# Copies and adding transfers in both halves of experts 2 to 6, expert 1's second weights made earlier, and 48 instead of 60 weight conversions ahead of the last layer

## The chip, the cores and the metric

The kernel runs on one core of a Trainium2 chip. The metric is device time in microseconds (us) of one execution. Everything else in this document comes from the hardware profiler's record of one execution: its engines are PE (TensorE: matmuls; PEld, its weight loads), DVE (VectorE), ACT (ScalarE), POOL (GpSimd) and SP (SyncE), which here issues nearly all DMA transfers. PEclk is the clock that TensorE was granted, as a share of its full speed.

## The reference, cut to what matters

```python
x = attention(q, k, v)                    # 4 x 576 tokens = 2304, 8 heads of 64: local and strided masks
logits = x @ w_gate; P = np.exp(logits - logits.max())
for _ in range(8):                        # Sinkhorn: rows, columns
    P /= P.sum(1, keepdims=True) + 1e-09
    P /= P.sum(0, keepdims=True) + 1e-09
    P *= N / E
for e in range(8):                        # experts: 512 -> 1024 -> 512
    out += P[:, e:e+1] * (np.maximum(x @ w1[e], 0) @ w2[e])
xn = out / sqrt(mean(out**2) + 1e-6) * rms_g
g = xn @ w_gate2; val = xn @ w_val        # 512 -> 1536
result = (g * sigmoid(g) * val) @ w_out   # 1536 -> 512
```

All of it is float32. The four SwiGLU weights arrive as float64 and are turned into float32 on the chip.

## The kernel before

**Products.** A float32 product is made of three matmuls on values split into a high and a low part (ACT copies the high part, DVE subtracts to get the low one). Experts 1 to 7 and the last layer use a scheme of seven products for a 2 x 2 block matrix (k = 0 to 6) in place of eight.

**Stages.** Attention ends at 253 us and overlaps expert 0, which is computed plainly in chunks of 256 tokens and a last one of 512 (matmuls L725 to L727) until 337 us. The gate and the Sinkhorn rows and columns (L702 to L720, with small matmuls L711) lie around the start of expert 1. Experts 1 to 7 follow, from 325.5 to 1673 us in 42 groups, then the SwiGLU layer in three passes, 18 groups.

**A group** is (expert g, half hh of the hidden features, third qd of the tokens). An expert has six groups: hh = 0 with qd = 0, 1, 2, then hh = 1 with qd = 2, 1, 0. In this text they are its first to sixth group. A group has two rounds of seven slots; a slot is one first-layer product (six matmuls, L1152, into one of two banks called ub) whose result DVE or ACT takes out of the bank (DVE: L1184, L1258, ACT: L1295, L1303), splits (ACT L1177, DVE L1180), and leaves for the second layer. Behind each slot stands one second-layer unit of nine matmuls (L1752, into banks called db), which belongs to the slot 12 slots earlier (LAG = 12). So the second layer of a group lies mostly in the time of the group that follows it, and that of an expert's sixth group in the first group of the next expert. The next product of a bank waits until the bank has been read.

**Second-layer results.** When the unit of product k is complete, `evict_1` takes it to the accumulator acc: by an ACT copy (L1773) for hh = 0 and k in (0, 2, 3, 4), else by a DVE add (L1784; k = 5 is a double one of 128x1536). When both halves of an expert are in acc, `close_region` weighs the region with the gate (ACT, L1803, three of them) and `gather` adds it to a buffer in HBM (L1809, a transfer with accumulation that POOL issues); the next expert's copy then waits for the transfer. Expert 7 gets that buffer back by an adding transfer into acc.

**Weights.** `second_weights` loads a half's second-layer weights into a tile raw_2 (L1038), forms differences (DVE L1041) and splits them (ACT L1054, DVE L1057) product by product, in the group before. raw_2 has the tag "r", the place that last_w (expert 0's last weights) holds before it.

**Float64 weights.** `conversion` turns them into float32 in 72 pieces. A piece is a 256 KB load (L824 or L827), seven DVE instructions in four steps (L832, L833; L839, L843; L849, L850; L856) and a store to HBM (L860). There is one buffer, cv: the load of the next piece is issued when L850 of this one has read it. The queue conv hands out steps with a fixed number of ticks between them (CONV_WAIT; a tick is a slot's worth of work); CONV_EP pieces are handed out from expert 2 on, the others from the second group of the first pass on. `prepare_2` for a SwiGLU pass calls conv.drain, which at that place writes down every piece that is still missing up to the one it needs, step behind step.

**The last layer** starts with the normed tokens: `norm_turn` and `norm_blocks` (L1395 to L1453) make them out of acc and write them to HBM (SP, L1429 and L1453), and SP loads them back as blocks xt and xx (L1084), one per product. An instruction list per engine is fixed when the kernel is built: every engine works through its own in order.

Of the kernel before, what the change touches and what calls it, by code (L numbers as in the profile page):

```python
# [17 lines left out]
P = 128  # L18
# [95 lines left out]
def kernel(  # L114
# [45 lines left out]
    EARLY = 2  # L160
    EARLY_AT = (5, 6)
    SUMS = 24
    CONV_WAIT = (7, 12)
    CONV_EP = 60
    LAG = 12
    TURN_AT = (29, 30, 31, 32, 33, 34), (32, 33, 34, 35, 36, 37)
    BLOCK_LAG = (2.5, 1.6, 0.85)
# [855 lines left out]
    def w2_piece(k, r, s):  # L1023
        return w2t.rearrange("p f s n -> p f (s n)")[:, k, 512 * r + 256 * s : 512 * r + 256 * (s + 1)]

    def second_weights(g, hh):

        both = const.tile([P, 2048], F32, name="raw_2", tag="r")
        raw = [both[:, 1024 * r : 1024 * (r + 1)] for r in range(2)]
        b11, b12, b21, b22 = ([t[:, 256 * i : 256 * (i + 1)] for t in raw] for i in range(4))  # L1030
        new = [fa[:, 4608 + 256 * r : 4864 + 256 * r] for r in range(2)]
        t1, t3, t2, t4 = new, b12, b11, b21

        def load(r):
            f = 2 * hh + r
            for h in range(2):
                rows = w2[g][(f + h * (NF // 2)) * P : (f + h * (NF // 2) + 1) * P, :]
                nc.sync.dma_start(out=raw[r][:, 512 * h : 512 * (h + 1)], in_=rows)  # L1038

        def sub(out, a, b):  # L1040
            nc.vector.tensor_tensor(out=out, in0=a, in1=b, op=ALU.subtract)  # L1041

        def early(r):
            sub(t1[r], b12[r], b11[r])
            sub(t3[r], b22[r], b12[r])
            return 600

        def late(r):
            sub(t2[r], b22[r], t1[r])
            sub(t4[r], b21[r], t2[r])  # L1050
            return 600

        def high(k, r):
            nc.scalar.activation(w2_piece(k, r, 0), (b21, b11, t4, t2, t1, t3, b22)[k][r], AF.Copy)  # L1054

        def low(k, r):
            nc.vector.tensor_tensor(  # L1057
                out=w2_piece(k, r, 1), in0=(b21, b11, t4, t2, t1, t3, b22)[k][r],
                in1=w2_piece(k, r, 0).bitcast(F32), op=ALU.subtract,
            )  # L1060
            return 256

        def begin():
            prep2.add([(WRITE, lambda: load(0)), (0, lambda: load(1))])

        def product(k):
            steps = []
            if k == 0:
                steps += [(READ, lambda: early(0)), (STEP, lambda: early(1))]
            steps += [(1, lambda: [high(k, r) for r in range(2)].clear()), (1, lambda: sum(low(k, r) for r in range(2)))]  # L1070
            if k == 1:
                steps += [(1, lambda: late(0)), (1, lambda: late(1))]
            prep2.add(steps, ("w2", g, hh, k))

        return begin, product
# [386 lines left out]
    with tc.manual_schedule():  # L1462
# [182 lines left out]

        def down_tile(u, t):
            u.down(u, t)
            if not u.left and t == u.n // P - 1 and u.f == NF - 1:
                begin_2[0], product_2[0] = second_weights(1, 0)
                begin_2[0]()  # L1650
                for k in range(7):
                    product_2[0](k)

        for idx in range(-LOOK, n1 - LOOK):
            nxt = idx + LOOK
# [7 lines left out]
            if u.f == 0:  # L1663
                if "x" not in u.cell:
                    fetch(u)
                if u.left:
                    bg.add(gate(u.t0, u.n, u.cell["x"]), 20)
                    if u.at:
                        area = fa[:, :1280], fa[:, 1280:3328].bitcast(F32R)
                        steps = sums(0, us[0].cell["x"], *area) if u.at == 1 else []  # L1670
                        steps += sums(u.at, u.cell["x"], *area)
                        bg.add(steps, 30 if u.at == 1 else SUMS, tag="sums")
                else:
                    bg.drain()
                    begin_sbuf()
                    area = acc[:, 2].rearrange("p a n -> p (a n)")[:, :1280], hx.rearrange("p a n -> p (a n)")[:, :2048]
                    wgc2 = hx.rearrange("p a n -> p (a n)")[:, 2048:2560].rearrange("p (c n) -> p c n", c=KC)
                    gate_split(wgc2)
                    steps = []
                    for i in range(2):  # L1680
                        x = [t[:, :, i * TA : (i + 1) * TA] for t in u.cell["x"]]
                        steps += sums(u.at + i, x, *area)
                    bg.add(steps, 40, tag="sums")
                    load_1(1, 0)
                    for k in (0, 1, 4, 3, 5, 2):
                        load_block(xmap[k], False, 0, k)
            u.up(u)
# [73 lines left out]
        def evict_1(n, k):  # L1761
# [6 lines left out]
                ps = ps[:, :, None, :].to_broadcast([P, 3, 2, 256])  # L1768
            else:
                a = a[:, :, 256 * col : 256 * (col + 1)]  # L1770
            if hh == 0 and k in (0, 2, 3, 4):
                bg.drain(("expert", qd, half, col if half else None))
                nc.scalar.copy(a, ps)  # L1773
            elif (g, hh) == (E - 1, 1):
# [12 lines left out]
            if n % NQD == NQD - 1:  # L1787
                if n < NGP - 1:
                    product_2[at](k)
                elif k >= 3:  # L1790
                    prepare_2(E, (0, 2, 1, 3)[k - 3])
            if hh == (g < E - 1) and k in (1, 5, 6):
                close_region(g, qd, *((1, 0) if k == 1 else (0, None) if k == 5 else (1, 1)))
            if (g, hh) == (E - 1, 1) and k >= 5:
                scales[k - 5].add(norm_scale(qd, 3 * (k - 5)), ("scale", qd))
# [171 lines left out]
        def fetch_left(k):  # L1967
            for x in list(left):
                if x[3] == k or made(x[2], x[3]):
                    norm.drain(("plain" if x[3] < 3 else "blocks", x[2]))  # L1970
                    load_block(*x)
                    left.remove(x)

        xmap, free = nmap, nfree
        free, gone_x = free[:1], free[1]
        last_r = const.tile([P, 2048], F32R, name="last_r", tag="r")
# [163 lines left out]
```

## Time and profile before

| | us |
|---|---|
| median of 3 runs | 2172.15 (2170.27 to 2173.97) |
| profiled execution | 2169.7 |
| its span in the trace | 2167.6 |

| engine | busy us | share of the span | instructions |
|---|---|---|---|
| PE | 2040.1 | 94% | 13611 |
| DVE | 1661.7 | 77% | 3601 |
| ACT | 1199.1 | 55% | 2800 |
| POOL | 194.8 | 9% | 232 |

The span is what the trace shows from the first to the last instruction; 2.1 us of the profiled execution's time lie around it. In the rows below, a row of windows has the stretch, its length, and then for PE, PEld, DVE, ACT and POOL the busy time and the number of instructions, at last PEclk, the share of time in which the 16 DMA engines were busy, and GB/s; a "sum" row adds the windows of one question. A row of the timeline has the start, the duration, engine, line, operation, out<-in, the count, and in brackets how long the engine had been idle and what released it. Durations of one instruction in a group are in ns.

### The profile page before, as it was taken

What the parts mean: (1) busy time and instruction counts of PE and PEld (TensorE: products, weight loads), DVE (VectorE), ACT (ScalarE), POOL (GpSimd) and SP (SyncE); (2) the same over time, 40 slices, a digit from 0 to 9 for tenths busy, and PEclk for the clock granted to TensorE, in tenths of its full rate; (3) what the DMA queues carried; (4) which work ended last, traced back from release to release, by engine and by line L of the source; (5) the groups of instructions that cost most, each with busy time, mean ns of one, the idle gap of its engine ahead of it and who ended that gap; (6) DMA issues with size and microseconds to landing.
All of it is one profiled execution on the core that took longest, in us unless ns stands there. A gap on an engine that the chain in (4) does not pass through costs nothing. (4 is left out here: it accounts for less than half of the span.)

```text
span 2167.6 us, 37111 instructions
## 1 busy us (share of the span) xinstructions
PE 2040.1 (94%) x13611; PEld 1939.6 (89%) x13611; DVE 1661.7 (77%) x3601; ACT 1199.1 (55%) x2800; POOL 194.8 (9%) x232
## 2 busy tenths in 40 slices
PE   8999997999999999999999999999997789999998
PEld 7888887999999899999989999999997678998897
DVE  4767646879899888989898898888788765667744
ACT  6856324666665655666565566656775444433322
POOL 6533200001000100100010010001100000000000
PEclk9999999999999999999999999999998889999999
DMA  7687675587737745683773677377764475243341
GB/s 189 173 223 197 186 237 189 190 280 170 250 129 212 197 171 189 164 255 131 210 212 127 216 177 243 132 206 201 186 214 141 136 228 170 81 152 114 124 158 58
DMA packets 319172, 391.20 MB, mean 180 GB/s; under 512 B 78800, under 2 KB 225168, under 8 KB 318992
## 3 DMA queue, kind: packets, MB, share of 16 engines
q1 hardware_dynamic: 298080, 353.52, 50.0%
q0 software_dynamic: 20912, 35.33, 9.7%
q8 instruction: 107, 1.75, 0.3%
q14 instruction: 73, 0.60, 0.1%
HBM read 294.41 MB, written 94.37 MB: 179 GB/s over the span
## 5 line engine op out<-in xcount | busy, mean ns | idle before, releaser
L1152 PE MATMUL ub<-xt,w1t 128*128 128x384 f32 x2328 | 477.6, 342 | 36.2 <-DMA xt<-xnd 15.7
L1152 PEld LDWEIGHTS ub<-xt,w1t 128*128 128x128 f32 x2328 | 401.2, 192 | 45.3 <-DVE fa L1184 18.4
L1152 PE MATMUL ub<-xx,w1t 128*128 128x384 f32 x1956 | 396.9, 340 | 14.3 <-DVE fa L1184 11.2
L1752 PE MATMUL db<-w2t,ht 128*128 128x256 f32 x2772 | 382.6, 283 | 7.6 <-DVE acc L1784 6.9
L1752 PEld LDWEIGHTS db<-w2t,ht 128*128 128x128 f32 x2772 | 369.5, 190 | 11.8 <-DVE acc L1784 10.8
L1752 PE MATMUL db<-w2t,hx 128*128 128x256 f32 x2520 | 352.0, 284 | 10.4 <-DVE acc L1784 5.5
L1152 PEld LDWEIGHTS ub<-xx,w1t 128*128 128x128 f32 x1956 | 334.9, 191 | 21.3 <-DVE fa L1184 13.6
L1752 PEld LDWEIGHTS db<-w2t,hx 128*128 128x128 f32 x2520 | 335.7, 191 | 20.0 <-DVE acc L1784 14.4
L1184 DVE TENSOR_TENSOR fa<-ub,fa 128x384 f32<-128x384 f32 x360 | 199.4, 554 | 164.3 <-PE ub L1152 147.9
L1303 ACT ACTIVATE fa<-fa 128x384 f32<-128x384 f32 x252 | 132.2, 525 | 284.4 <-DVE fa L1184 283.9
L1784 DVE TENSOR_TENSOR acc<-db,acc 128x768 f32<-128x768 f32 (+1 forms) x189 | 211.5, 1119 | 41.2 <-PE db L1752 39.9
L1180 DVE TENSOR_TENSOR ht<-fa,ht 128x384 fp32r<-128x384 f32 x344 | 189.4, 551 | 25.1 <-ACT ht L1177 24.5
L1180 DVE TENSOR_TENSOR hx<-fa,hx 128x384 fp32r<-128x384 f32 x316 | 174.4, 552 | 33.6 <-ACT hx L1177 31.8
L1177 ACT ACTIVATE ht<-fa 128x384 fp32r<-128x384 f32 x344 | 177.3, 517 | 32.0 <-DVE fa L1355 31.1
L1295 ACT COPY fa<-ub 128x384 f32<-128x384 f32 x252 | 119.4, 474 | 127.0 <-PE ub L1152 124.3
L1177 ACT ACTIVATE hx<-fa 128x384 fp32r<-128x384 f32 x316 | 163.0, 520 | 47.6 <-DVE fa L1355 44.1
L1258 DVE TENSOR_TENSOR fa<-fa 128x384 f32<-128x384 f32 x336 | 185.3, 551 | 5.1 <-ACT fa L1299 1.7
L1809 POOL DMA_DIRECT2D y1d<-acc x54 | 62.3, 1154 | 1173.1 <-ACT acc L1803 698.8
L1320 ACT COPY fa<-ub 128x384 f32<-128x384 f32 x108 | 51.6, 478 | 109.9 <-PE ub L1152 109.8
L1803 ACT ACTIVATE acc<-acc,prob 128x256 f32<-128x256 f32 (+1 forms) x189 | 102.5, 572 | 11.9 <-DVE acc L1784 11.7
L916 DVE TENSOR_TENSOR w1t<-fa,w1t 128x256 fp32r<-128x256 f32 (+1 forms) x170 | 88.5, 524 | 10.3 <-ACT w1t L913 10.2
L913 ACT ACTIVATE w1t<-fa 128x256 fp32r<-128x256 f32 (+1 forms) x170 | 80.6, 495 | 2.1 <-DVE fa L919 2.1
(251 smaller groups left out, 3069.6 us busy)
## 6 DMA issues: line engine op xcount, KB each, us to landing
xt<-xdt SPq DMA_DIRECT2D x111, 768.0 KB
xx<-xdt SPq DMA_DIRECT2D x92, 768.0 KB
xt<-xnd SPq DMA_DIRECT2D x25, 768.0 KB
xx<-xnd SPq DMA_DIRECT2D x24, 768.0 KB
fa<-in_moe_w_dram SPq DMA_DIRECT2D x56, 256.0 KB
raw<-in_moe_w_dram SPq DMA_DIRECT2D x56, 256.0 KB
y1d<-acc POOLq DMA_DIRECT2D x36, 384.0 KB, 6.4
y1d<-acc POOLq DMA_DIRECT2D x18, 768.0 KB, 9.3
```

The lines of the kernel that those rows point to most:

```text
L913: nc.scalar.activation(at(k, n), src, AF.Copy)
L916: nc.vector.tensor_tensor(out=at(7 + k, n), in0=src, in1=at(k, n).bitcast(F32), op=ALU.subtract)
L1152: nc.tensor.matmul(ps[:, :TH], w[i][:, c], x[:, k, c], start=first and c == 0 and n == 0, stop=c == 1 and n == 2, skip_group_check=True,)
L1177: nc.scalar.activation(h[0], src, func)
L1180: engine.tensor_tensor(out=h[1], in0=src, in1=h[0].bitcast(F32), op=ALU.subtract)
L1184: nc.vector.tensor_tensor(out=out, in0=ps, in1=more, op=ALU.add)
L1258: nc.vector.tensor_tensor(**kw)
L1295: nc.scalar.copy(z[nm], ps)
L1303: nc.scalar.activation(z[nm], z[nm], AF.Relu)
L1752: nc.tensor.matmul(spot(k, m), hm[x], w[y], start=BEGIN[k] and r == 0 and m in FIRST[PAIR[k]] and i == 0, stop=r == 1 and i == 2, skip_gro ...
L1784: nc.vector.tensor_tensor(out=a, in0=ps, in1=a, op=ALU.add)
L1803: nc.scalar.activation(a, a, AF.Copy, scale=prob[:, tile_of(qd, b), g : g + 1])
```

## The change

Experts 2 to 6 (E_STD < g < E - 1, with E_STD = 1 and E = 8): the second half opens with ACT copies where it had DVE adds, and the first half is closed like the second, with weighing and adding transfers. Expert 1's second weights are loaded into acc[:, 1] at the start of expert 0's last chunk and made product by product behind its first seven columns of downs. 48 instead of 60 conversion pieces go into the experts and 24 instead of 12 into the passes, with 11 and 6 ticks between them instead of 7 and 12. What remains in the queue of norm blocks for the first pass's third of the tokens is written down ahead of that pass.

```diff
-    CONV_WAIT = (7, 12)
-    CONV_EP = 60
+    CONV_WAIT = (11, 6)
+    CONV_EP = 48
...
-    def second_weights(g, hh):
+    def second_weights(g, hh, both=None):
...
-        both = const.tile([P, 2048], F32, name="raw_2", tag="r")
+        if both is None:
+            both = const.tile([P, 2048], F32, name="raw_2", tag="r")
...
             u.down(u, t)
-            if not u.left and t == u.n // P - 1 and u.f == NF - 1:
-                begin_2[0], product_2[0] = second_weights(1, 0)
-                begin_2[0]()
-                for k in range(7):
-                    product_2[0](k)
+            if not u.left and t == u.n // P - 1 and u.f < 7:
+                product_2[0](u.f)
...
                     load_1(1, 0)
+                    begin_2[0], product_2[0] = second_weights(1, 0, acc[:, 1].rearrange("p a n -> p (a n)")[:, :2048])
+                    begin_2[0]()
                     for k in (0, 1, 4, 3, 5, 2):
                         load_block(xmap[k], False, 0, k)
...
-            if hh == 0 and k in (0, 2, 3, 4):
+            if (hh == 0 or E_STD < g < E - 1) and k in (0, 2, 3, 4):
                 bg.drain(("expert", qd, half, col if half else None))
                 nc.scalar.copy(a, ps)
...
-            if hh == (g < E - 1) and k in (1, 5, 6):
+            if (hh == (g < E - 1) or E_STD < g < E - 1) and k in (1, 5, 6):
                 close_region(g, qd, *((1, 0) if k == 1 else (0, None) if k == 5 else (1, 1)))
...
+        norm.drain(("blocks", passes[0][1]))
         xmap, free = nmap, nfree
```

From the function second_weights on every line number of the changed kernel is one higher than that of the kernel before (L1184 becomes L1185); lines above stay.

**The seventh group of the passes** (where prepare_2 asks for weights of the last pass). This is what stands on DVE of the kernel before around the eviction of the second product (L1184 with ub_4232, the bank that the fourth product takes next); no conversion is near.

```order
L1180 TENSOR_TENSOR ht<-fa,ht 128x384
L916 TENSOR_TENSOR xt<-fa,last_r 128x512
L919 TENSOR_TENSOR fa<-fa 128x256
L1184 TENSOR_TENSOR fa<-ub_4232,fa 128x384
L919 TENSOR_TENSOR fa<-fa 128x256
L1341 TENSOR_TENSOR fa<-fa 128x384
L916 TENSOR_TENSOR xt<-fa,last_r 128x512
```

And this is the same place on DVE of the changed kernel: the first and the last rows of the stretch of conversion pieces.

```order
L919 TENSOR_TENSOR fa<-fa 128x256
L839 TENSOR_SCALAR cv<-cv 128x256
L843 SCALAR_TENSOR_TENSOR cv<-cv 128x256
L849 TENSOR_SCALAR cv<-cv 128x256
L850 SCALAR_TENSOR_TENSOR cv<-cv 128x256
L856 TENSOR_TENSOR cv<-cv 128x256
L832 TENSOR_SCALAR cv<-cv 128x256
L833 TENSOR_SCALAR cv<-cv 128x256
...
L856 TENSOR_TENSOR cv<-cv 128x256
L1185 TENSOR_TENSOR fa<-ub_4266,fa 128x384
L1342 TENSOR_TENSOR fa<-fa 128x384
```

Where the dots stand, the seven rows of a piece are repeated: the piece begun before is finished and five whole pieces follow it, each with its own load, ahead of the eviction of the second product's bank (L1185 with ub_4266). Behind it six more pieces follow, in three pairs within two groups.

**The start of expert 1.** On DVE of the kernel before, the weight differences (L1041, out of raw_4315) and the Sinkhorn steps stand ahead of the eviction of a product (L1184).

```order
L720 TENSOR_SCALAR prob<-prob 128x144
L1041 TENSOR_TENSOR fa<-raw_4315 128x256
L1041 TENSOR_TENSOR raw_4315<-raw_4315 128x256
L702 TENSOR_REDUCE cv<-prob 128x18
L703 TENSOR_SCALAR cv<-cv 128x18
L704 RECIPROCAL cv<-cv 128x18
L705 TENSOR_TENSOR prob<-prob,cv 128x144
L708 TENSOR_REDUCE cv<-prob 128x8
L1258 TENSOR_TENSOR fa<-fa 128x384
```

In the changed kernel the same Sinkhorn step stands there without weight differences; the last split of a weight (L1058) follows it.

```order
L720 TENSOR_SCALAR prob<-prob 128x144
L916 TENSOR_TENSOR w1t<-fa,w1t 128x256
L702 TENSOR_REDUCE cv<-prob 128x18
L703 TENSOR_SCALAR cv<-cv 128x18
L704 RECIPROCAL cv<-cv 128x18
L705 TENSOR_TENSOR prob<-prob,cv 128x144
L708 TENSOR_REDUCE cv<-prob 128x8
L1058 TENSOR_TENSOR w2t<-acc,w2t 128x256 x2
L1185 TENSOR_TENSOR fa<-ub_4265,fa 128x384
```

All eight differences and the other splits have moved to places beside expert 0's last chunk.

**The start of the passes.** On SP of the kernel before, three block loads (L1084) and two weight loads (L984) stand between the stores of two norm blocks.

```order
L1429 DMA xnd<-norm_r 128x6x128 x2
L1084 DMA xt<-xnd 128x2x768 x2
L1084 DMA xx<-xnd 128x2x768
L984 DMA fa<-m2v 128x512 x2
L1453 DMA xnd<-norm_r 128x4x128
L1453 DMA xnd<-fa 128x4x128
L1453 DMA xnd<-acc 128x2x128
L1453 DMA xnd<-cv 128x4x128
L1453 DMA xnd<-acc 128x2x128
L1084 DMA xt<-xnd 128x2x768 x2
L1084 DMA xx<-xnd 128x2x768 x2
```

In the changed kernel the five stores stand first and all seven loads behind them.

```order
L1430 DMA xnd<-norm_r 128x6x128 x2
L1454 DMA xnd<-norm_r 128x4x128
L1454 DMA xnd<-fa 128x4x128
L1454 DMA xnd<-acc 128x2x128
L1454 DMA xnd<-cv 128x4x128
L1454 DMA xnd<-acc 128x2x128
L1085 DMA xt<-xnd 128x2x768 x2
L1085 DMA xx<-xnd 128x2x768
L1085 DMA xt<-xnd 128x2x768 x2
L1085 DMA xx<-xnd 128x2x768 x2
L984 DMA fa<-m2v 128x512 x2
```

What moved is the second block's work: its four ACT and four DVE steps (L1419, L1420) too stand ahead of the first loads. PE's own list is the same in both kernels at these three places.

## Rows read from the trace of the kernel before

**Rows 1.** Windows of the five first groups, experts 3 to 7: first, and their sum.

```profile
710.20:747.10 36.90, 32.53 (x213) 31.39 (x212) 35.72 (x80) 23.53 (x57) 3.45 (x3) 0.95 0.79 224
...
sum 178.20, PE 158.71 PEld 153.50 DVE 173.91 ACT 116.58 POOL 17.27; mean PE 31.74 PEld 30.70 DVE 34.78 ACT 23.32 POOL 3.45
```

**Rows 2.** Windows of the five fourth groups, experts 2 to 6: their sum.

```profile
sum 166.90, PE 156.42 PEld 151.78 DVE 156.45 ACT 111.19 POOL 0.00; mean PE 31.28 PEld 30.36 DVE 31.29 ACT 22.24 POOL 0.00
```

**Rows 3.** Windows: fourth group of expert 7; second group of expert 3.

```profile
1564.70:1594.50 29.80, 29.80 (x212) 29.48 (x211) 27.88 (x60) 25.94 (x61) 3.45 (x3) 1.00 0.70 198
747.10:777.00 29.90, 29.90 (x213) 29.58 (x212) 22.02 (x46) 16.05 (x32) 1.28 (x1) 1.00 0.81 249
```

**Rows 4.** Timeline of PE, 724 to 745 us: start, us, line, count, idle before.

```profile
727.46 1.97 PE L1152 MATMUL ub<-xt,w1t 128*128 128x384 f32 x6 [1.89 <-DVE fa L1184]
...
743.78 1.34 PE L1752 MATMUL db<-w2t,ht 128*128 128x256 f32 x9 [0.79 <-DVE acc L1784]
```

**Rows 5.** Groups of instructions by form, 500 to 1500 us: xcount, busy, mean ns.

```profile
L1784 DVE TENSOR_TENSOR acc<-db,acc 128x768 f32<-128x768 f32 x129 | 122.9, 953 | 13.9 <-PE db L1752 13.1
...
L1057 DVE TENSOR_TENSOR w2t<-raw,w2t 128x256 fp32r<-128x256 f32 x130 | 48.9, 417 | 1.3 <-ACT w2t L1054 1.2
...
L1773 ACT COPY acc<-db 128x768 f32<-128x768 f32 x60 | 48.0, 801 | 17.1 <-PE db L1752 17.0
L1803 ACT ACTIVATE acc<-acc,prob 128x256 f32<-128x256 f32 x97 | 45.9, 501 | 1.1 <-DVE acc L1784 0.9
...
L1803 ACT ACTIVATE acc<-acc,prob 128x512 f32<-128x512 f32 x50 | 34.1, 714 | 9.5 <-DVE acc L1784 9.5
```

**Rows 6.** Page, DMA queue and issues of the adding transfers.

```profile
q0 software_dynamic: 20912, 35.33, 9.7%
...
y1d<-acc POOLq DMA_DIRECT2D x36, 384.0 KB, 6.4
```

**Rows 7.** Timeline of DVE, 337 to 354 us.

```profile
346.68 0.42 DVE L1041 TENSOR_TENSOR fa<-raw 128x256 f32<-128x256 f32 x1 [3.76 <-DMA raw<-in_moe_w_dram]
```

**Rows 8.** Timeline of PE, 337 to 365 us.

```profile
352.82 0.59 PE L711 MATMUL ub<-cv,ones 128*128 128x8 f32 x2 [8.33 <-DVE fa L1184]
353.27 4.19 PE L1152 MATMUL ub<-xx,w1t 128*128 128x384 f32 x12
```

**Rows 9.** Windows around the start of expert 1.

```profile
295.00:325.00 30.00, 30.00 (x138) 24.11 (x137) 15.74 (x41) 7.92 (x17) 0.00 (x0) 1.00 0.46 128
353.00:364.10 11.10, 10.82 (x52) 10.62 (x52) 10.74 (x32) 6.76 (x18) 0.00 (x0) 0.72 0.63 196
```

**Rows 10.** Timeline of PE, 1665 to 1692 us.

```profile
1673.14 2.29 PE L1152 MATMUL ub<-xt,w1t 128*128 128x384 f32 x6 [5.77 <-DMA xt<-xnd]
...
1689.14 2.26 PE L1152 MATMUL ub<-xt,w1t 128*128 128x384 f32 x6 [9.88 <-DMA xt<-xnd]
```

**Rows 11.** Timeline of SP, the same stretch.

```profile
1668.84 0.87 SPq L1084 DMA_DIRECT2D xt<-xnd  x2
...
1677.62 0.37 SPq L1453 DMA_DIRECT2D xnd<-norm_r  x1
...
1684.73 0.87 SPq L1084 DMA_DIRECT2D xt<-xnd  x2
```

**Rows 12.** Timeline of PE and DVE, 2010 to 2013 us.

```profile
2010.15 0.55 DVE L1184 TENSOR_TENSOR fa<-ub,fa 128x384 f32<-128x384 f32 x1
...
2011.04 2.25 PE L1152 MATMUL ub<-xx,w1t 128*128 128x384 f32 x12
```

**Rows 13.** Timeline of SP and DVE, 2040 to 2047 us.

```profile
2040.18 0.33 SPq L824 DMA_DIRECT2D cv<-in_moe_w_out_dram  x1
...
2044.29 0.29 DVE L832 TENSOR_SCALAR cv<-cv 128x256 uint32<-128x256 uint32 x1
...
2046.05 0.42 DVE L850 SCALAR_TENSOR_TENSOR cv<-cv 128x256 f32<-128x256 uint32 x1
```

**Rows 14.** DMA activity, 2040 to 2044 us, in 40 slices of 0.1 us.

```profile
GB/s 0 0 0 0 0 0 0 0 0 0 0 82 205 205 143 143 164 287 307 287 277 348 328 379 328 154 113 92 82 10 0 0 0 0 0 0 0 0 0 0
```

## The prediction

> **What bounds the kernel now.** I read the busy times first: PE 94%, DVE 77%, ACT 55% of the span, so PE's own work sets most of the time, and this change leaves PE's work as it is. What can move is PE's idle time. So I cut the span into the groups of the experts and passes and looked at each group's length. Most groups of the experts take 29.9 us with PE busy throughout [rows 3]. The first groups of experts 3 to 7 take 178.2 us for five, 35.6 each, with DVE busy 173.9 of it: here DVE is the bound [rows 1]. The fourth groups of experts 2 to 6 take 166.9 us, 33.4 each, with DVE 156.5 [rows 2]. In the timeline of PE the waits there end with L1184 or L1784, both DVE [rows 4]. The other holes are the start of expert 1 (8.33 us of idle PE, [rows 8]) and the start of the passes (5.77 and 9.88 us, [rows 10]). The passes themselves have little idle PE: in the seventh group the product's eviction L1184 starts at 2010.15 us and PE needs the bank again after six of the twelve matmuls that begin at 2011.04 and take 2.25, so at about 2012.2 [rows 12]. The eviction ends at 2010.7: 1.5 us of slack.
>
> The sum is made against the profiled execution's own 2169.7 us (span 2167.6, and 2.1 around it). That is 2.45 us under the median of the runs, 0.1%.
>
> **Part 1: copies and closings in experts 2 to 6.** 60 evictions (5 experts, 3 thirds, 4 products) leave DVE, 0.953 us each, and go to ACT at 0.801 [rows 5]. DVE loses 57 us in all, but it pays only where DVE sets the end. The second layer lags by 12 of 14 slots, so the second halves' adds lie in fourth to sixth groups and in the next expert's first group. The fifth and sixth stand at 29.9 us already, and the second groups too [rows 3]; nothing is to be had there. The first group of the next expert holds three of them: 3 x 0.953 = 2.86 us of a DVE that is full, in five groups: 14.3 us. The excess over 29.9 in these groups is 178.2 - 149.4 = 28.8 us, the bound from above. A check from nearby: the fourth groups have DVE at 31.3 instead of 34.8 us and take 33.4 instead of 35.6, so 3.5 us of DVE less went with 2.3 us of time; at that rate 2.86 gives 1.85 a group, 9.4 us in all. I take 12, between 9.4 and 14.3, nearer to the latter since these groups follow DVE closely.
>
> The price: 15 closings more. Each is six weighs of 0.50 and three of 0.714 us on ACT, 5.1 us [rows 5], in the second to fourth groups, 76.5 us of ACT in all. ACT is at 22.2 of 33.4 us in the fourth groups [rows 2]. The fourth group of expert 7 has 25.9 of 29.8 us of ACT and 27.9 of DVE and no stall [rows 3]. So I cost it at nothing, covered by ACT's idle third; were that cover gone, the weigh stands in ACT's list ahead of splits (L1177) that DVE waits for, one or two of them late by 1.5 us (three weighs) a group, 15 groups, 22 us at most.
>
> The gathers are 45 adding transfers more, per closing two of 384 KB and one of 768 KB, 1.57 MB. On their queue 35.33 MB took 9.7% of 16 engines' span [rows 6], 210 us, 6.0 us per MB, so a closing takes 9.4 us of all engines. A second group has the DMA engines busy 81% of 29.9 us [rows 3]; a closing's 31% on top give 1.12. A first group carries loads and three gathers at 79% [rows 1], and the waits of PE in its rows are for DVE [rows 4]. The Trainium skill, page "DMA: Bandwidth & Descriptors", section "Issuing engines are not separate DMA queues", says that transfers issued by scalar, sync and gpsimd engines run on the same 16 DMA engines and interleave. By that rule the gathers delay SP's x loads, and it speaks against the change: 0.12 x 29.9 is 3.6 us in each of five groups, 18 us, an estimate; by the first groups' row it is nothing. No second group of before has a closing, so the trace decides neither.
>
> I take nothing for the gathers, by the first groups, which are nearest, and keep 18 us as the other bound. The copies wait for their region's gather: 6.4 us to landing at the median [rows 6]; a copy comes a group later.
>
> **Part 2: where the conversions lie.** A piece is 2.19 us of DVE from L832's start to L850's end (2044.29 to 2046.05 + 0.42 = 2046.47), and L856 behind it. 12 pieces fewer in the experts relieve DVE by 26 us, spread over 31 groups of which ten are bound by it, so at most 8; but the list of the changed kernel puts a piece into the first slots of expert 2's first group, where none was, about 2 us. I take 1 us of gain.
>
> In the passes the twelve pieces more are the core of the forecast. In the seventh group the list of DVE has one piece's end and five whole pieces ahead of the eviction L1184 of the second product. There is one buffer: the load of a piece is issued at L850's end. The load issued at 2040.18 [rows 13] shows in the DMA activity to 2043.0, the store of the piece before being part of it [rows 14]: 2.8 us. So a piece behind a piece takes 2.8 + 2.2 = 5.0 us, and five take 25. PE's fourth product has 1.5 us of slack and gets the bank 25 us later; all that is behind it on PE's list waits, downs too. That is 25 - 1.5 + 1 (end of the first piece and L856) = 24.5 us. After such a hole PE runs at a lower clock: at expert 1's start, after 8.33 us of idle PE, twelve matmuls took 4.19 us [rows 8] against 2.25 at full clock [rows 12], and the window after it had PEclk 0.72 [rows 9], so 11.1 x 0.28 = 3.1 us. I add 3. The pairs behind it: the second piece of a pair has its load issued only when the first has ended, 2.2 + 2.8 + 2.2 = 7.2 us in a row on DVE, less about 3 us of slack: 4 for the first pair, less where other steps lie between, 10 for the three. Part 2 in the passes: 24.5 + 3 + 10 = 37.5. From below: if the store is what stretches the DMA activity, the load is 1.9 (2041.1 to 2043.0), a piece 4.1, and five 20.5; without the pairs 23. From above, loads that meet x blocks as long as half of the 5 us period: 45.
>
> **Part 3: expert 1's second weights.** Before, L1041 waits 3.76 us for its load [rows 7] and eight differences (0.42) stand in DVE's list ahead of L1184, whose end releases PE after 8.33 us [rows 8]. In the changed list no difference is left there, and one product's two splits (2 x 0.417) are. Ahead of it go 3.76 + 4 x 0.42 + 0.59 of a second short wait = 6.0 us, so the hole falls from 8.33 to about 2.3. The lower clock after it (3.1 us, above) goes to half, and ten more splits (0.417 each) leave the next 20 us, where PE stood for 3 us; of these I take 1.5. Sum: 6 + 1.5 + 1.5 = 9. The work goes to 285 to 333 us, where DVE is busy 15.7 of 30 us and ACT 7.9, PE fully [rows 9]; 8 x 0.42 + 14 x 0.417 = 9.2 us find room. Bounds: 5 (only the wait and the differences) and 12.
>
> **Part 4: the norm blocks first.** Loads for the first three products were issued at 1668.84, the stores of the second block from 1677.62, and the other loads at 1684.73 [rows 11]; PE waited 5.77 for the first and 9.88 for the fourth product [rows 10]. Now four ACT and four DVE steps of about 0.4 us and five stores stand ahead of the first loads: they come 3.3 us later, at 1672.1, the first product at 1676.4, and the fourth load lands four blocks on. 249 GB/s at a DMA share of 0.81 [rows 3] is 307 at a full one, 2.6 us for 786,432 bytes, so 1672.1 + 4.3 + 3 x 2.6 = 1684.2. So the fourth begins at 1684 rather than 1689.1: 5 us gained. Bounds: 0 (loads of one block wait for the last store's landing) and 9.
>
> **Sum.** -12 (experts) - 1 + 37.5 - 9 - 5 = +10.5. 2169.7 + 10.5 = 2180.2 us, 0.5% slower. A difference of 0.2%, 4.3 us, is about what a measurement of this kernel can tell from none.
>
> **The rivals.** (A) This forecast: the conversions outweigh the rest; the gains' terms give 21 to 41 us and the conversions cost 23 to 45, mostly 2173 to 2192 in all. Chance 0.55.
> (B) The pairs are hidden (0 in place of 10) and the first groups give 14: +10.5 - 10 - 2 = -1.5, 2168, no change. For it: DVE has slack in the passes (20.4 of 25.4 us in the seventh group). Against: lists are in order, so idle time later doesn't help the product that waits. Chance 0.2.
> (C) Faster: the experts' groups bound by DVE close to 29.9. Then 28.8 us in the first and up to 17 in the fourth groups come back, together 46 in place of 13: 2169.7 - 46 + 37.5 - 14 = 2147; at two thirds of it 2162. The place is the first seven slots, where DVE runs behind and hands the delay from slot to slot; the waits there are 1.89 and 0.79 us in one group [rows 4]. It decides once the experts give over 28 us: 37.5 - 9 - 5 - 28 = -4.5. For it: five first groups at 35.6, of which DVE takes all but 0.9 us each; against: three adds less leave DVE at 32, still above 29.9. Chance 0.2.
> (D) Slower still: weighs on ACT or gathers cost in the second to fourth groups, 22 or 18 us as above: about 2200. Against: expert 7's fourth group. Chance 0.05.
>
> By these, slower by over 0.2% (above 2176.5) 0.56, D and all but a little of A; within 0.2% 0.2, B; faster 0.24, C and the tail of A. The range 2158 to 2195 takes in B and the nearer half of C; A's own is 2172 to 2192.
>
> **What would show it.** In the seventh group of the passes a single hole in PE of 20 to 28 us released by the eviction L1184 (L1185 in the new count), and L832 on DVE idle about 2.8 us each, released by the load of cv; if the hole is under 10, the step on the load is wrong. The five first groups at 33 us in place of 35.6; at 30, C is right. ACT copies waiting for gathers or PE for xt would show D. PE's hole at expert 1's start at 2 to 3 us, and at the passes' start one hole of 9 and no second. The forecast is wrong if pieces in a row overlap load and work, or if the experts give more than 25 us.

## The result and the profile after

| | before | changed |
|---|---|---|
| median of 4 runs | 2172.22 us (2170.27 to 2173.97) | 2189.14 us |
| ratio | | 1.0076, 95% interval 1.0056 to 1.0095 |
| profiled execution, its span | 2169.7, 2167.6 | 2189.38, 2187.4 |

The changed kernel is 0.8% slower, as forecast in direction (2180.2 us, range 2158 to 2195) and above the forecast in size: 16.9 us between the medians and 19.7 between the two profiled executions, where the sum gave 10.5. One of the changed kernel's four executions took 5049.90 us; its cause is not known, and the ratio leaves it out.

The page of the changed kernel shows the work that was moved: DVE 40 us less, ACT 105 us more, and the adding transfers' queue at 16.3% instead of 9.7% [rows 6]. PE's busy time is within 0.3 us of before, 2040.1.

```profile
PE 2039.8 (93%) x13611; PEld 1938.9 (89%) x13611; DVE 1622.0 (74%) x3541; ACT 1303.8 (60%) x2995; POOL 246.1 (11%) x277
...
q0 software_dynamic: 35072, 58.93, 16.3%
...
PE 16%; DVE 5%; DMA 3%; ACT 1%; issue 1%; SPq 0%; DVEq 0%; ACTq 0%
```

The last of these is the chain that ended last, by engine. DMA had 1% of it before and has 3% now. Where it waits is seen in the windows of the changed kernel: the seventh and eighth group of the passes, then the first groups of experts 3 to 7 (one and the sum of five), the sum of the fourth groups of experts 2 to 6, and two second groups.

```profile
1972.30:2039.10 66.80, 30.41 (x122) 27.07 (x121) 38.36 (x95) 10.64 (x23) 0.00 (x0) 0.69 0.24 75
2039.10:2076.90 37.80, 26.46 (x122) 24.13 (x121) 23.20 (x56) 9.23 (x20) 0.00 (x0) 0.86 0.39 134
...
706.70:740.50 33.80, 31.09 (x212) 29.93 (x212) 32.14 (x76) 25.92 (x61) 3.45 (x3) 1.00 0.85 247
...
sum 162.50, PE 153.80 PEld 149.03 DVE 155.51 ACT 129.50 POOL 17.27; mean PE 30.76 PEld 29.81 DVE 31.10 ACT 25.90 POOL 3.45
...
sum 161.10, PE 154.08 PEld 150.04 DVE 151.47 ACT 129.14 POOL 17.27; mean PE 30.82 PEld 30.01 DVE 30.29 ACT 25.83 POOL 3.45
...
740.50:770.40 29.90, 29.90 (x213) 29.58 (x212) 20.06 (x40) 20.19 (x42) 3.45 (x3) 1.00 0.90 249
925.60:955.40 29.80, 29.80 (x212) 29.48 (x211) 20.40 (x42) 20.12 (x41) 3.45 (x3) 1.00 0.94 261
```

The five first groups take 162.5 us where they took 178.2 [rows 1], the fourth 161.1 where they took 166.9 [rows 2], and the second groups, which now carry a closing, still take 29.9 [rows 3]. All of that and more is lost in two groups: 66.8 and 37.8 us, where the kernel before needs 25.4 and 24.4:

```profile
2007.50:2032.90 25.40, 23.25 (x121) 21.23 (x121) 20.42 (x44) 10.49 (x23) 0.00 (x0) 1.00 0.29 88
2032.90:2057.30 24.40, 23.26 (x121) 21.30 (x120) 18.05 (x42) 9.42 (x21) 0.00 (x0) 1.00 0.38 136
```

The timeline of PE in the two groups of the changed kernel has these holes:

```profile
2005.42 2.29 PE L1153 MATMUL ub<-xx,w1t 128*128 128x384 f32 x6 [27.41 <-DVE fa L1185]
...
2022.99 4.21 PE L1153 MATMUL ub<-xx,w1t 128*128 128x384 f32 x12 [6.11 <-DVE fa L1342]
...
2048.99 1.01 PE L1153 MATMUL ub<-xx,last_r 128*128 128x384 f32 x2 [5.19 <-DVE fa L1185]
...
2065.43 3.96 PE L1153 MATMUL ub<-xx,w2t 128*128 128x384 f32 x12 [6.15 <-DVE fa L1342]
```

and DVE's timeline in the first of them shows what stands ahead of the eviction L1185:

```profile
1977.41 0.42 DVE L850 SCALAR_TENSOR_TENSOR cv<-cv 128x256 f32<-128x256 uint32 x1
...
1980.81 0.29 DVE L832 TENSOR_SCALAR cv<-cv 128x256 uint32<-128x256 uint32 x1 [2.51 <-DMA cv<-in_moe_w_val_dram]
...
1982.61 0.42 DVE L850 SCALAR_TENSOR_TENSOR cv<-cv 128x256 f32<-128x256 uint32 x1
...
1986.21 0.29 DVE L832 TENSOR_SCALAR cv<-cv 128x256 uint32<-128x256 uint32 x1 [2.72 <-DMA cv<-in_moe_w_val_dram]
...
2004.81 0.55 DVE L1185 TENSOR_TENSOR fa<-ub,fa 128x384 f32<-128x384 f32 x1
```

As in the prediction, "seventh group of the passes" is the seventh pair of pass and third of the tokens; each pair has two of the 18 groups that the passes are cut into, and the expectations call these two the seventh and eighth. Other groups of the passes are named by their time below; where the last expectation says third and sixth, it counts singly.

This is the forecast's picture: each piece's load is released by L850 of the piece before, DVE idles until it has landed, and the product's eviction stands behind all of them.

The start of expert 1 and the start of the passes, on PE of the changed kernel:

```profile
310.60 0.27 PE L684 MATMUL db<-ident,cv 128*1 128x128 f32 x1 [1.46 <-DVE cv L681]
...
349.04 0.60 PE L711 MATMUL ub<-cv,ones 128*128 128x8 f32 x2 [2.47 <-DVE fa L1185]
349.49 4.19 PE L1153 MATMUL ub<-xx,w1t 128*128 128x384 f32 x12
353.48 3.18 PE L1153 MATMUL ub<-xt,w1t 128*128 128x384 f32 x12
...
1651.95 2.29 PE L1153 MATMUL ub<-xt,w1t 128*128 128x384 f32 x6 [11.53 <-DMA xt<-xnd]
```

The hole of 8.33 us is 2.47 now, but the matmuls behind it are as slow as before [rows 8], and there is a new wait of 1.46 us ahead, in expert 0's last chunk. At the passes' start one hole of 11.5 us stands in place of 5.77 and 9.88 [rows 10].

### The profile page after: what moved, and what is told of

It reads as the page before. It is cut to its first block, busy times and chain, and to the rows that moved or that the text cites. A ratio compares the mean times of both kernels' runs of the same rounds, so it can differ in the third digit from the quotient of the medians.

```text
span 2187.4 us, 37495 instructions
## 1 busy us (share of the span) xinstructions
PE 2039.8 (93%) x13611; PEld 1938.9 (89%) x13611; DVE 1622.0 (74%) x3541; ACT 1303.8 (60%) x2995; POOL 246.1 (11%) x277
## 3 DMA queue, kind: packets, MB, share of 16 engines
q1 hardware_dynamic: 298080, 353.52, 49.8%
q0 software_dynamic: 35072, 58.93, 16.3%
## 5 line engine op out<-in xcount | busy, mean ns | idle before, releaser
L1153 PE MATMUL ub<-xx,w1t 128*128 128x384 f32 x1956 | 398.7, 341 | 40.6 <-DVE fa L1185 30.7
L1185 DVE TENSOR_TENSOR fa<-ub,fa 128x384 f32<-128x384 f32 x360 | 199.7, 555 | 194.4 <-PE ub L1153 179.3
L1809 POOL DMA_DIRECT2D y1d<-acc x99 | 114.2, 1153 | 1094.4 <-ACT acc L1803 480.2
L1803 ACT ACTIVATE acc<-acc,prob 128x256 f32<-128x256 f32 (+1 forms) x324 | 176.0, 572 | 15.7 <-DVE acc L1784 15.5
L1784 DVE TENSOR_TENSOR acc<-db,acc 128x768 f32<-128x768 f32 (+1 forms) x129 | 154.4, 1197 | 40.8 <-PE db L1752 39.6
L1773 ACT COPY acc<-db 128x768 f32<-128x768 f32 x144 | 115.1, 799 | 21.4 <-PE db L1752 18.6
```

Source lines behind the costliest of these rows:

```text
L1153: nc.tensor.matmul(ps[:, :TH], w[i][:, c], x[:, k, c], start=first and c == 0 and n == 0, stop=c == 1 and n == 2, skip_group_check=True,)
L1185: nc.vector.tensor_tensor(out=out, in0=ps, in1=more, op=ALU.add)
L1784: nc.vector.tensor_tensor(out=a, in0=ps, in1=a, op=ALU.add)
L1803: nc.scalar.activation(a, a, AF.Copy, scale=prob[:, tile_of(qd, b), g : g + 1])
L1809: nc.gpsimd.dma_start(out=y, in_=t, accum_op=ALU.add)
```

## The experiments

All ratios are to the kernel before, run beside it on the same chip. Where the text speaks of the experts' groups, it means those from expert 2's first to expert 7's first.

| run | median us | ratio, 95% interval |
|---|---|---|
| conversions as before, all other parts | 2147.10 | 0.9894 (0.987 to 0.9918) |
| conversions alone | 2221.19 | 1.0224 (1.0197 to 1.025) |
| second weights alone | 2168.21 | 0.9979 (0.9965 to 0.9994) |
| copies and closings alone | 2159.78 | 0.9942 (0.992 to 0.9963) |
| norm blocks alone | 2167.33 | 0.9968 (0.9951 to 0.9984) |
| three pieces in a row | 2181.36 | single run, no ratio |
| pieces without loads | 2178.87 | single run, no ratio |
| 54 pieces, 9 and 3 ticks | 2148.09 | 0.9894 (0.9876 to 0.9912) |
| 54 pieces, 10 and 3 ticks | 2154.43 | 0.9921 (0.9902 to 0.994) |
| 60 pieces, 8 and 12 ticks | 2142.39 | 0.9848 (0.9819 to 0.9876) |
| no added closings | 2142.89 | 0.9853 (0.9826 to 0.988) |
| pieces begun three groups earlier | 2140.22 | 0.9844 (0.9828 to 0.9861) |

The theory is the forecast's: conversions in a row cost more than the other three parts give. Its main rival is that the hole in the passes has another cause, or that it takes all the parts together.

**The changed kernel with the conversions as before.**

```diff
-    CONV_WAIT = (11, 6)
-    CONV_EP = 48
+    CONV_WAIT = (7, 12)
+    CONV_EP = 60
```

> The changed kernel with the conversions as before: 60 pieces in the experts, 7 and 12 ticks between them. Theory: in the trace of the changed kernel everything up to the seventh group of the passes is 35 us earlier than before, and the seventh and eighth group alone give back 55; if the rows of conversion pieces are the cause, both groups are at 24 to 25 us again and the time is 2134 to 2142. Rival: a good part of what the experts gained came from the wider spacing of the pieces there, not from the copies; then the five first groups of experts 3 to 7 stand above 34 us instead of 32.5, and the time is 2142 to 2155. Second rival: the hole in the passes has another cause (weights or blocks that come late); then it stays at 20 us or more and the time is above 2160.

Its windows for the seventh and eighth group of the passes are those of before:

```profile
1986.90:2012.30 25.40, 23.25 (x122) 21.26 (x121) 20.40 (x44) 10.47 (x23) 0.00 (x0) 1.00 0.29 89
2012.30:2036.60 24.30, 23.15 (x121) 21.25 (x120) 17.97 (x42) 9.33 (x21) 0.00 (x0) 1.00 0.38 138
```

So the two numbers make the hole, and the other three parts together make the kernel 1.1% faster. The time, 2147, is in the first rival's range (experts gained from the spacing too) and not in the theory's 2134 to 2142. The rival holds in part: the experts' groups take 966.9 us here and 961.7 in the changed kernel, though the first groups are not above 34 us at the mean (33.1). The rest lies ahead of expert 2, where this edit changes nothing: this execution reaches expert 1 at 330.8 us (the others between 324.8 and 330.3) and expert 2 at 524.2, where the changed kernel is at 516.8.

**The kernel before with the conversions alone.** The edit is the first one of the change's diff, nothing else.

> The kernel before with the numbers of the conversions alone changed (48 pieces, 11 and 6 ticks). Theory: the hole comes with the numbers alone, 27 us in the seventh group and three smaller ones behind it; the two groups cost 55 us, and twelve pieces fewer in the experts give back 5 to 10: 2216 to 2224. Rival: the pieces stand in a row only together with the other parts, or cost less where PE comes to them later; then 2175 to 2200.

The hole is the same, 27.55 us, on PE of this kernel:

```profile
2038.65 2.29 PE L1152 MATMUL ub<-xx,w1t 128*128 128x384 f32 x6 [27.55 <-DVE fa L1184]
```

The two groups take 67.6 and 38.1 us, 56 more than before, and the time is 48 us longer. The rival that it needs the other parts falls. The experts gave 6 us back: the experts' groups take 975.5 instead of 981.5, all of it in the five fourth groups (159.8 instead of 166.8).

**Expert 1's second weights alone.** The edits are second_weights' argument, down_tile and the call beside load_1.

> The kernel before with expert 1's second weights made early, and nothing else. Theory: the hole of 8.33 us at expert 1's start falls to 2 to 3, expert 1 begins 2 us later since the weights share DVE with expert 0's last chunk, net gain 5 us: 2166 to 2168. Rival by the prediction: nothing is lost ahead of 325 us, gain 9: 2162 to 2164. Rival the other way: what is gained at the start is given back in expert 1's next groups; within 1.5 us of before.

About 5 us less (1 to 8 by the interval), the theory's. Expert 1's first two groups take 65.2 us where they took 72.6, and expert 1 begins 1.5 us later, at 327.0, behind a wait of 1.88 us of PE for the gate's L681, as in the changed kernel.

**Copies and closings alone.** The edits are the two conditions in evict_1.

> The kernel before with the copies and closings of experts 2 to 6 alone. Theory of the prediction: three adds fewer in five first groups give 9 to 14 us, closings cost nothing: 2157 to 2163. Second theory, by the trace of the changed kernel: the fourth groups gain too (DVE has adds fewer at their start), 16 to 22 us: 2150 to 2156. Rival: ACT's weighs and the gathers cost in the second to fourth groups as long as pieces stand densely, gain below 5: above 2167.

The time is inside the first range. By the windows the five first groups give 12.9 us (sum 165.3) and the fourth groups 1.2 (sum 165.6), and the experts' groups 14.5 in all (967.0 instead of 981.5). The second theory, that the fourth groups gain by the copies, falls: in the changed kernel they gain by the conversions' numbers, as the run with the conversions alone shows.

**Norm blocks alone.** The edit is the line norm.drain.

> The kernel before with the norm blocks of the first pass's tokens written down ahead of the pass, and nothing else. Theory by the prediction: the second hole of 9.88 us goes, the first grows by 3 to 5: 5 us gained, 2165 to 2168. Rival: the loads behind the stores are all later and give it back in the following products: within 2 us of before.

7 us in the median, 5.5 of it in one place: the groups from expert 7's sixth to the second of the passes take 133.7 us instead of 139.2.

**Three whole pieces in a row instead of five.**

```diff
-    CONV_WAIT = (11, 6)
+    CONV_WAIT = (11, 3)
```

> The changed kernel with 3 instead of 6 ticks between the pieces in the passes: 14 pieces instead of 12 are done ahead of the seventh group, and 3 whole pieces instead of 5 stand in front of the eviction of its second product. Theory: a whole piece in a row costs 5.3 us (load 2.9 behind the one before, work 2.4), so the hole of 27.4 us falls to 16.8 and the time by 10 to 11 us, to 2177 to 2180. Rival: the hole is one wait for something else (a weight or a block); then it stays near 27 and the time within 3 us of 2189.

On PE of this kernel the hole is

```profile
1995.14 2.29 PE L1153 MATMUL ub<-xx,w1t 128*128 128x384 f32 x6 [14.34 <-DVE fa L1185]
```

13.1 us shorter. In the changed kernel all five pieces lie in the hole whole (26.6 us). Here two do (10.6 us); the load of the first of the three was issued before PE ran dry, and 2.8 us of that piece lie in the hole. The time falls by 8 rather than 10 to 11 us, since pieces at this pace cost 6 us in a group of the passes ahead (30.7 us at 1873 us, 24.7 in the changed kernel). The hole follows the number of pieces.

**Pieces in the passes without their loads.**

```diff
-                conv.add([(STEP, whole), (1, convert(*items[n + 1])[0]), (2, store)], tag)
+                conv.add([(STEP, whole), (1, convert(*items[n + 1])[0] if wait > 6 else lambda: None), (2, store)], tag)
```

> The changed kernel, but in the passes only the first of the 24 pieces loads its float64 values; the others convert what stands in the buffer, so most of the last weights are wrong. Theory, that the load behind the piece before is more than half of a piece's price: without it a piece is 2.7 us of DVE, the hole falls from 27.4 to 14 us and the pairs behind it by 2.5 us each: 2166 to 2172. Rival: the store takes the load's place, since the next piece writes the values it stores (store 1.7 us, then six steps): a piece is 4.1 us, the hole 21 us: 2177 to 2182.

The rival is right: the hole is 21.58 us, and DVE of this kernel waits in each piece for the store of the one before.

```profile
1975.71 0.29 DVE L832 TENSOR_SCALAR cv<-cv 128x256 uint32<-128x256 uint32 x1
1977.50 0.29 DVE L833 TENSOR_SCALAR cv<-cv 128x256 f32<-128x256 f32 x1 [1.49 <-DMA m2v<-cv]
...
1979.86 0.29 DVE L832 TENSOR_SCALAR cv<-cv 128x256 uint32<-128x256 uint32 x1
```

4.15 us a piece. So the load is the longer of two waits that lie side by side: taking the loads away, with one buffer for the values read and one for those written, got back only 1.2 of 5.3 us a piece.

**54 pieces in the experts, 9 or 10 ticks there, 3 in the passes.**

```diff
-    CONV_WAIT = (11, 6)
-    CONV_EP = 48
+    CONV_WAIT = (9, 3)
+    CONV_EP = 54
```

> The changed kernel with 54 pieces in the experts (9 ticks) and 18 in the passes (3 ticks): all pieces are done before a drain asks for them, by the instruction list. Theory: no hole in the seventh group (under 26 us long), and the wider spacing in the experts gives a part of the 9 us that 48 pieces gave there: 2138 to 2145. Rival: what matters there is where a piece falls, not how many; then the same as with 60 pieces, 2145 to 2149. Second rival: six pieces more in the passes cost there what they give in the experts: above 2149.

> As the run before with 10 ticks in the experts: the pieces there end later, two of them in expert 7. Theory: spacing decides, 2 to 4 us better than 9 ticks: 2134 to 2142. Rival: place decides: up to 4 us worse.

With 9 ticks the first rival is right, it is the time of 60 pieces: 966.1 us in the experts' groups, against 966.9 there, and 5 us more in the group of the passes at 1882 us (29.2 instead of 24.5). The seventh group has no hole, though at 27.8 us it is longer than the theory's 26. The run with 10 ticks is outside both of its forecasts: the experts' groups take 964.6 us, 2.3 less than with 60 pieces, but the last piece falls into expert 7's fourth group and stands there with all its steps in a row; the window is 37.1 us instead of 29.9, with one hole of 4.67 us on PE behind an L832 that waits 3.03 us for its load.

```profile
1545.50:1582.60 37.10, 32.43 (x213) 31.90 (x212) 30.95 (x69) 26.25 (x62) 3.45 (x3) 0.91 0.73 205
```

This load was issued at 1542.80 us, 7.4 us before L832 starts at 1550.23, where the loads of the changed kernel's hole need 3.1. Beside it run the adding transfers that bring expert 7 its sum back (1152 KB issued in this time; their queue has 71% of the 16 engines from 1542.5 to 1550.5 us). That they make it slow is likely, but no run takes them away.

**60 pieces with 8 ticks.** The edit is CONV_WAIT = (8, 12) and CONV_EP = 60 in the changed kernel.

> The first experiment's kernel with 8 instead of 7 ticks between the pieces in the experts: still 60 there, the last four of them in expert 7's second and third group, where DVE has 8 to 10 us to spare, and the passes as before. Theory that the spacing of the pieces in the groups that DVE sets counts: 3 to 6 us better than 7 ticks, 2141 to 2145. Rival that the place of single pieces decides, either way: 2144 to 2150.

The median is in the theory's range, but the experts' groups say otherwise: 967.0 us with 8 ticks, 966.9 with 7. What differs from the first run lies ahead of expert 2 (reached at 518.2 us, there at 524.2), so the two are not told apart; both beat the kernel before and the changed one clearly.

**Without the added closings.**

```diff
-            if (hh == (g < E - 1) or E_STD < g < E - 1) and k in (1, 5, 6):
+            if hh == (g < E - 1) and k in (1, 5, 6):
```

> The first experiment's kernel (all parts but the numbers of the conversions), but without the added closings: the first half of experts 2 to 6 is neither weighed nor added to the buffer and is overwritten by the second half's copies, so half of these experts is missing from the output. It shows what 135 weighs and 45 adding transfers cost. Theory: nothing, ACT and the DMA engines have room: within 3 us of that kernel's 2147. Rival by the rule on DMA engines: transfers delay loads, 18 us: 2127 to 2133. Rival on ACT: splits come late in the third and fourth groups: 2130 to 2142, with the fourth groups shorter by 1 to 2 us.

The median is 4.2 us under that of the first run, 1.2 more than the theory allows. But the edit acts from expert 2 on, and there little is gained: the experts' groups take 965.7 us, against 966.9 with the closings. The rest lies ahead, where expert 2 is reached at 515.5 us instead of 524.2. In a second group (without, then with, the first run's kernel) ACT loses 4 us and the DMA share 0.10, and the length stays:

```profile
736.10:765.90 29.80, 29.80 (x212) 29.48 (x211) 21.96 (x46) 16.07 (x32) 1.28 (x1) 1.00 0.81 248
```

```profile
745.20:775.00 29.80, 29.80 (x212) 29.48 (x211) 21.93 (x46) 20.16 (x42) 3.45 (x3) 1.00 0.91 261
```

By these two executions 135 weighs and 45 adding transfers cost 1.2 us, which is less than the experts' groups of kernels that are alike there differ by (958.5 to 961.7 in four). Both rivals fall: there is no 18 us, and the fourth groups take 165.5 us against 165.6.

**Pieces of the passes begun three groups earlier.**

```diff
+                conv.limit = 0
                 conversion(conv_items[CONV_EP:], CONV_WAIT[1])
...
-    CONV_WAIT = (11, 6)
+    CONV_WAIT = (11, 5)
```

> The changed kernel with its 48 pieces in the experts, but the 24 in the passes begin in the third group of the passes instead of the sixth: their queue no longer waits for the builder's own estimate that DVE has room (limit 0 from there on), with 5 ticks between them. By the instruction list every piece is done before a drain asks for it. Theory: the 55 us of the seventh and eighth group come back and the experts keep what the wider spacing gave: 2132 to 2140, better than 60 pieces. Rival: pieces in the third to fifth groups, at 47 to 62% of DVE, delay evictions in a list worked through in order, or their loads meet the block loads there: 10 us or more of it is lost again, 2144 to 2155. Second rival: the hole was late weights, not the row of pieces: above 2170.

The pieces now share the buffer cv with norm blocks that run until 1777 us, so some of the converted and some of the normed values are wrong in this run; the work done is the same. The median is at the upper end of the theory's range and under the rival's. The seventh and eighth groups:

```profile
1977.10:2004.90 27.80, 25.12 (x122) 22.67 (x121) 23.24 (x54) 10.65 (x23) 0.00 (x0) 0.94 0.18 57
2004.90:2027.80 22.90, 22.90 (x121) 21.34 (x120) 16.40 (x37) 9.39 (x21) 0.00 (x0) 1.00 0.54 197
```

The two take 50.7 us (49.8 before), and the time is 49 us less than the changed kernel's at the same 48 and 24 pieces. So not the number of pieces in the passes but that they come late and in a row is the cost. A start behind the last norm block was not tried. Of the kernels here that do the whole work, 60 pieces with 8 ticks have the lowest time; 60 with 7 and 54 with 9 ticks follow with the same ratio.

## Why the prediction was right, point by point

| step of the sum | forecast | changed kernel, from the windows | the part alone |
|---|---|---|---|
| conversions in the passes | +37.5 | +54.8 (66.8 + 37.8 - 25.4 - 24.4) | +56 |
| copies and closings | -12 | together -19.8 (981.5 to 961.7) | -14.5 |
| conversions in the experts | -1 | (in the row above) | -6.0 |
| expert 1's second weights | -9 | -5.2 (-7.3 in three groups, start 2.1 later) | -5 |
| norm blocks first | -5 | -5.3 (139.2 to 133.9 in three groups) | -7 |

With 4.9 us less in the groups that no row names (mostly the third and the eleventh of the 18 groups of the passes, 26.2 and 24.5 us where they took 28.3 and 27.0), this makes the 19.6 us between the ends of PE's work in both traces.

The direction and what brings it about were right. That the total came within 9 us is in part luck: the conversions' term was 17 us too small and the experts' gains 7 too small, the second weights' gain 4 too large, and 5 us came from groups that the sum does not name. The gains, 35 us, are within the 21 to 41 that the rivals' paragraph uses; how these follow from the parts, whose own bounds add up to 14 and 43, the prediction does not say.

**Conversions in the passes.** The mechanism, the place and the count were right; the size was not, and 54.8 us lie outside the bounds of 23 to 45. The hole is 27.4 us in place of 24.5: five pieces take 26.6 us instead of 25, the end of the first piece and L856 1.9 instead of 1, and the slack was 1.1 instead of 1.5. A piece in a row takes 5.3 us rather than 5.0 because the load, from issue to L832, is 2.9 to 3.2 us, where the DMA activity of one load gave 2.8 [rows 14]. The three pairs cost 6.1, 5.2 and 6.2 us of idle PE, 17.5 in place of 10: a pair is 7.9 us in a row on DVE with its last L856 (7.2 in the forecast), and 1.7 to 2.7 us of it were hidden, not 3 and more. And the lower clock was priced once (3 us), but slow matmuls stand behind every one of the four holes: in the two groups PE is busy 30.4 and 26.5 us, where the kernel before needs 23.25 and 23.26 for the same work, 10.4 us more. These three, 2.9, 7.5 and 7.4 us, are the 17 us.

**Copies and closings.** 14.5 us alone, in the first groups as said (12.9), near the upper of the two estimates: 2.86 us of DVE a group came back nearly whole, since these groups follow DVE. The check by the fourth groups (9.4) was the weaker guide. With DVE at 155.5 of 162.5 us in the changed kernel it sets the first groups still, as said against rival C.

**What the closings cost.** Nothing, as taken, by the experiment without them. The Trainium skill, page "DMA: Bandwidth & Descriptors", section "Issuing engines are not separate DMA queues", has these transfers interleave with SP's on the same engines. The trace agrees: the share of the 16 engines is 0.90 and 0.94 in second groups with them, 0.81 without [rows 3]. The 18 us made from it do not come: PE is busy all of 29.9 us there. The price of a transfer was right: without the closings the share is 0.66 over 966 us of experts, with them 0.81, which is 145 us for 23.6 MB, 6.1 us per MB (taken as 6.0). Wrong was to put a closing's whole work into the second group: there the share rises by 0.10, and from 0.35 to 0.68 in the third group and from 0.50 to 0.78 in the fourth, where the engines had room.

**Conversions in the experts** were mis-sized the other way: 6 us, not 1, and all of it in the fourth groups, where DVE is busy 156.5 of 166.9 us [rows 2]. The number of pieces there is not what counts: the five fourth groups hold 10 before and 9 in the changed kernel, and the run with 54 pieces and 9 ticks has 9 too, at 165.2 us instead of 161.1. The place is: in the 70 fourth groups of experts 2 to 6 in these fourteen traces, those whose first piece begins 12 to 17 us behind the group's start take 30.8 to 32.55 us, and all others, with a first piece earlier or later, 32.57 to 35.1. No run moved a single piece, so this is a regularity of the traces and not yet a tested cause. It fits the spacings: the experts' groups take 966.9, 967.0, 966.1 and 964.6 us with 7, 8, 9 and 10 ticks, and 958.5 to 961.7 in the four kernels with 11.

**Expert 1's second weights.** Two steps were off. That the work "finds room" beside expert 0's last chunk: PE waits 1.5 to 1.9 us for L681 (the maximum over the gate's logits), which stands behind differences and splits on DVE. And that the lower clock goes to half with the hole: it stayed whole. The fall of the hole itself, 8.33 to 2.47, was worked out to 0.2 us; its sum takes four differences, as many as stand ahead of that eviction in the trace, where the sentence before it says eight. The start, 2.1 us later here, differs between executions: 324.8 to 326.8 us in the four runs with the weights as before, 325.8 to 330.8 in the ten with them made early.

**Norm blocks.** As forecast in kind: one hole, later (11.5 us, forecast 9), and no second.

Rival B is out, as no pair was hidden. Rival C's price, 28 us from the experts, was not reached (19.8). D is out by the run without closings.

## What to carry to other kernels

Moving work out of a crowded stage is worth what the crowded stage gives back only if it still meets its deadline where it goes: a queue that is emptied by force puts all that is late in one row of an in-order engine, and with a single buffer each element then costs load, work and all, 5.3 us here instead of 2.7 of engine time. Look in the instruction list for the longest such row ahead of an instruction that another engine waits for, and count each later pair at nearly its full length, with the slow clock behind each hole. Gains of parts that act on different stretches added up here (14.5 and 6.0 alone, 19.8 together), so parts can be kept and dropped singly: without the two numbers of the conversions the same change is 1.1% faster, not 0.8% slower.

## What the runs showed of the hardware that was not expected

At the start of expert 1 PE's clock did not depend on how long the last hole was in the way the forecast had it. Behind 8.33 us of idle PE twelve matmuls took 4.19 us [rows 8], and behind 2.47 us they took 4.19 as well, at a granted clock of 0.50 from 349.0 to 353.0 us, the lower of its two levels. PE had been busy 0.7 us of the 9.0 ahead in the first case (344 to 353 us) and 5.3 of 9.0 in the second (340 to 349 us). The window behind the second has this, against a clock of 0.72 before [rows 9]:

```profile
349.00:360.10 11.10, 11.06 (x54) 11.06 (x55) 7.43 (x22) 4.41 (x9) 0.00 (x0) 0.71 0.81 261
```

So shortening this hole gave back its idle time but none of the slow time after it, 3 us. And 23.6 MB more of adding transfers delayed nothing that PE waited for, not even in the two second groups with the DMA engines at 0.90 and 0.94; the one load here that took 7.4 us beside such transfers (54 pieces, 10 ticks) is a sign that this need not hold everywhere.
